# Loading the last block of w_out in a decode layer: four GpSimd transfers to ten of the DMA engines, in place of MLP rows and a side transfer

## The chip, the cores and the metric

The kernel runs on one core of one Trainium2 chip. The metric is the time of one execution on the device, in microseconds (us), as the median of several runs. Before the change it is 678.6 us, the median of three runs that lie between 678.34 and 678.68 us. A core has five instruction engines (TensorE or PE for matrix products, VectorE or DVE, ScalarE or ACT, GpSimd or POOL, SyncE or SP) and 16 DMA engines that carry all data between HBM and the on-chip memory SBUF.

## The reference, cut to what matters

One decode step: attention over a cached K and V, gated by a small MLP, both computed from the same normalised input.

```python
# B=8, D=512, Hq=32, Hkv=8, Sk=4096, Dh=128, Fh=896, one new position
xn = _layernorm(x, axis=-1)
s = _A_ref(xn, k_cache, v_cache, wq, wo)     # softmax(q k^T / sqrt(Dh)) v, then @ wo
z = gelu(xn @ w_in)                          # 512 -> 2*896
z1, z2 = z[..., :Fh], layernorm(z[..., Fh:])
g = silu((z1 * (w_sp * z2 + b_sp)) @ w_out)  # 896 -> 512
return x + s * g
```

All data are float32. The two caches hold 2 x 8 x 8 x 4096 x 128 numbers, 268 MB of the 291 MB that one execution reads.

## The kernel before, in words

**Buffers.** Three slots of 128 partitions x 16384 numbers, `slot_A`, `slot_B` and `slot_C` (8 MB each), take everything that is large. First `slot_B` takes wq, `slot_C` the MLP's weights and `slot_A` half of the first head's K. Then the eight heads follow (L645): for each, K in two halves into A and B, V in two halves into C and B. At the end wo goes into A in seven pieces, each smaller than the last or as large (`WO_PIECES`).

**Queues.** SP issues nearly all transfers, in program order: wq (L365), the side transfer (L371), then K, V and wo. An issue waits on SP until TensorE has freed the slot; the transfers themselves queue behind each other, so that there is as a rule a second one waiting when the first ends. ACT issues the input x in two parts (L362) and the MLP's weights (L368). GpSimd issues none. The hardware cuts a transfer over 128 partitions into rows, one for each partition, eight rows for each of the 16 DMA engines.

**The MLP's weights.** `w_in` (512 x 1792) and `w_out` (896 x 512) lie on the host as one array of 128 rows, `w_mlp`. `w_out` consists of `NB` = 7 blocks of 128 rows, each 512 columns; `LAST` is block 6. `w_mlp` holds w_in, the blocks 0 to 5, and of block 6 the first 256 columns: 10496 numbers in a row. The other 256 columns of block 6 come apart, as `w_ext`: 8 groups (`XG`) of 4 rows (`XR`), 32 rows of 1024 numbers (4 KB), which land on partitions 0 to 31 of `slot_C` behind the MLP's rows. So block 6's right half lies there in four chunks (`XC`) of 32 rows of w_out each.

**What uses them.** `mlp()` multiplies by w_in (L469), does gelu, norm and gate on VectorE, transposes the result u (L502) and multiplies by w_out (L514). For the right half of block 6, u's last columns are transposed once more in four chunks of 32 (L509), copied by VectorE (L510), and multiplied by the four chunks (L518). With the last of these products the MLP's use of `slot_C` ends: SP then issues the first V half into it (L596). VectorE copies y out of PSUM (L520).

**GpSimd** does little: a few constants at the start, a power for the first norm (L422) and one for the MLP's norm (L496), and for each head a copy of q (L543). Its program begins with one control instruction (`ISA`, in the table of its order below), before and after the change.

**Order.** Nothing is scheduled by a planner: each engine's instructions stand in the order in which the code issues them; a recorder (`Recorder`, `plan`) adds the waits on semaphores. A transfer with a key, such as `slots["C"]`'s, is waited for by TensorE at its first use; one without a key, such as the side transfer, has a semaphore of its own.

Of the kernel before, what the change touches and what calls it, by code (L numbers as in the profile page):

```python
# [15 lines left out]
P = 128  # L16
B, D = 8, 512
HKV, REP, S, DH = 8, 4, 4096, 128
NK = D // P
G = 4  # L20
J = S // (G * P)
R = 32
FH = 896
FQ = 256
NB = FH // P
# [11 lines left out]
E = 2  # L37
W = P // E
BANK = 512
XG, XR, XN = 8, 4, 256  # L40
XK = XG * XR
XC = P // XK
LAST = NB - 1


class Region:
# [297 lines left out]
        return self.rec.add(self.eng, "tensor_tensor", (out, a, b), {"op": ALU.subtract})  # L344


def gqa_gmlp_decode(real, x, kT, v, wq, wo, w_mlp, w_ext, out):
    nc = Recorder(real)

    def sb(name, shape, **kw):  # L350
        return real.alloc_sbuf_tensor(name, shape, F32, **kw).ap()

    def psum(name, shape):
        return real.alloc_psum_tensor(name, shape, F32).ap()

    slots = {n: sb(f"slot_{n}", [P, SLOT], align_bytes=ALIGN) for n in "ABC"}
    pbuf = sb("pbuf", [P, J * P])
    tbuf = sb("tbuf", [P, B * J * G * REP])
# [5 lines left out]

    nc.sync.dma_start(slots["B"], wq, key="B")  # L365
    wq_sb = slots["B"].rearrange("p (k n) -> p k n", k=NK)
    n_in, n_mlp = NK * 2 * FH, NK * 2 * FH + NB * D - XN
    nc.scalar.dma_start(slots["C"][:, :n_mlp], w_mlp, key="C")  # L368
    w_in_sb = slots["C"][:, :n_in].rearrange("p (k n) -> p k n", k=NK)
    ext = slots["C"][:XK, n_mlp:n_mlp + XC * XN]  # L370
    nc.sync.dma_start(ext, w_ext[:, :XR])  # L371
    w_ext_sb = ext.rearrange("p (c d) -> p c d", d=XN)

    def w_out_sb(j):
        return slots["C"][:, n_in + j * D:min(n_in + (j + 1) * D, n_mlp)]

    ident = sb("ident", [P, P])
    make_identity(nc, ident)
# [27 lines left out]
    def shift(t, i):  # L406
        lo = (E - 1 - i) * B
        return t[:, lo:lo + R]

    sc = psum("sc", [P, 2, 512])  # L410
    o_ps = [psum(f"o_ps{i}", [P, G, DH]) for i in range(2)]
    po = psum("po", [P, 512])[:, :B * REP]
    scr = [psum(f"scr{i}", [P, 512]) for i in range(3)]
# [6 lines left out]
    nc.vector.bn_aggr(mv, st)  # L420
    nc.vector.tensor_scalar(rstd[:, 0:1], mv[:, 1:2], EPS, None, op0=ALU.add)
    nc.gpsimd.tensor_tensor(rstd[:, 1:2], rstd[:, 0:1], neg_half[:B, 0:1], op=ALU.pow)  # L422
    nc.vector.tensor_scalar(xn, x_sb, mv[:, 0:1], rstd[:, 1:2], op0=ALU.subtract, op1=ALU.mult)
    pt = scr[0][:, :NK * B]
    for k in range(NK):
# [5 lines left out]
    for i in range(E):  # L431
        for g in range(G):
            lo = g * P + i * W
            nc.tensor.matmul(px[R * g:R * (g + 1), :W], shift(same8, i)[:B], x_sb[:, lo:lo + W],
                             start=(i == 0), stop=(i == E - 1))
# [21 lines left out]
    def mlp():  # L457
        zu = pbuf.rearrange("p (a f) -> p a f", f=FQ)
        z, u = zu[:, :2], zu[:, 2:]
        hT = tbuf[:, :2 * P].rearrange("p (a s) -> p a s", a=2)  # L460
        y_sb, e = tbuf[:, 2 * P:2 * P + D], zu[:, 2, :W]
        pz = scr[1]
        nc.vector.memset(pz, 0.0)
        for part in range(2):
            for k in range(NK):
                for g in range(G):
                    lo = g * FQ
                    n = min(FQ, FH - lo)
                    nc.tensor.matmul(pz[R * g:R * (g + 1), part * FQ:part * FQ + n], xnT[:, k, :],  # L469
                                     w_in_sb[:, k, part * FH + lo:part * FH + lo + n],  # L470
                                     start=(k == 0), stop=(k == NK - 1))
        zf, uf = z.rearrange("p a f -> p (a f)"), u.rearrange("p a f -> p (a f)")
        nc.vector.tensor_copy(zf, pz)
        nc.vector.tensor_mul(uf, zf, zf)
        nc.vector.tensor_scalar(uf, uf, 0.044715, 1.0, op0=ALU.mult, op1=ALU.add)
        nc.vector.tensor_mul(uf, uf, zf)
        nc.scalar.activation(uf, uf, AF.Tanh, scale=GELU_C)
        nc.vector.tensor_scalar(uf, uf, 1.0, 0.5, op0=ALU.add, op1=ALU.mult)
        nc.vector.tensor_mul(zf, uf, zf)

        def mean(src, pm, name):
            part_sum, t = sb(f"{name}_sum", [P, 1]), sb(name, [P, 1])
            nc.vector.tensor_reduce(part_sum, src, op=ALU.add, axis=AX.X)
            nc.tensor.matmul(pm, same_all, part_sum, start=True, stop=True)
            nc.vector.tensor_scalar(t, pm, 1.0 / FH, None, op0=ALU.mult)
            return t

        z1, z2 = z[:, 0, :], z[:, 1, :]
        mu = mean(z2, scr[0][:, :1], "mu")
        nc.vector.tensor_scalar(z2, z2, mu, None, op0=ALU.subtract)  # L490
        nc.vector.tensor_mul(u[:, 0, :], z2, z2)
        nc.vector.memset(u[(G - 1) * R:, 0, FH - (G - 1) * FQ:], 0.0)
        var = mean(u[:, 0, :], scr[2][:, :1], "var")
        nc.vector.tensor_scalar(var, var, EPS, None, op0=ALU.add)
        rs = sb("rs", [P, 1])
        nc.gpsimd.tensor_tensor(rs, var, neg_half, op=ALU.pow)  # L496
        nc.vector.tensor_scalar(z2, z2, rs, None, op0=ALU.mult)
        nc.vector.tensor_scalar(z2, z2, wb[:, 0:1], wb[:, 1:2], op0=ALU.mult, op1=ALU.add)
        nc.vector.tensor_mul(u[:, 1, :], z2, z1)
        th = scr[0][:, :2 * P]  # L500
        for a in range(2):
            nc.tensor.transpose(th[:, a * P:(a + 1) * P], u[:, 1, a * P:(a + 1) * P], ident)  # L502
        nc.vector.tensor_copy(hT.rearrange("p a s -> p (a s)"), th)
        low = R * (LAST // 2)
        hX = tbuf[:XK, 2 * P + D:2 * P + D + XC * R].rearrange("p (c r) -> p c r", r=R)
        tx = scr[2][:XK, :XC * R].rearrange("p (c r) -> p c r", r=R)
        for c in range(XC):
            lo = (LAST % 2) * P + c * XK
            nc.tensor.transpose(tx[:, c, :], u[low:low + R, 1, lo:lo + XK], ident[low:low + R, low:low + R])  # L509
        nc.vector.tensor_copy(hX, tx)  # L510
        for j in range(NB):
            g = j % G
            w_j = w_out_sb(j)
            nc.tensor.matmul(sc[R * g:R * (g + 1), 0, :w_j.shape[1]], hT[:, j % 2, R * (j // 2):R * (j // 2 + 1)],  # L514
                             w_j, start=(j < G), stop=(j + G >= NB and j < LAST))
        g = LAST % G
        for c in range(XC):
            nc.tensor.matmul(sc[R * g:R * (g + 1), 0, D - XN:], hX[:, c, :], w_ext_sb[:, c, :],  # L518
                             start=False, stop=(c == XC - 1))
        nc.vector.tensor_copy(y_sb, sc[:, 0, :])  # L520
        py = scr[2][:, :W]
        for i in range(E):
            for g in range(G):
                lo = g * P + i * W
                nc.tensor.matmul(py[R * g:R * (g + 1), :], shift(same8, i), y_sb[:, lo:lo + W],
                                 start=(i == 0), stop=(i == E - 1))
        nc.vector.tensor_scalar(e, py, -1.0, 87.0, op0=ALU.mult, op1=ALU.min)
        nc.scalar.activation(e, e, AF.Exp)
        nc.vector.tensor_scalar(e, e, 1.0, None, op0=ALU.add)
        nc.vector.reciprocal(e, e)  # L530
        nc.vector.tensor_mul(gate, py, e)
# [7 lines left out]
    p = pbuf.rearrange("p (j s) -> p j s", j=J)  # L539
# [101 lines left out]
    project_q(0)  # L641
    project_q(1)
    mlp()
    nc.meet("tensor")
    for h in range(HKV):  # L645
# [9 lines left out]
    for i in range(E):  # L655
        for g in range(G):
            lo = g * P + i * W
            nc.tensor.matmul(acc[R * g:R * (g + 1), :], shift(same8, i), part_sb[:, lo:lo + W],
                             start=False, stop=False)
# [43 lines left out]
```

## Time and profile before

The times of one execution, as the profiler took it:

| | |
|---|---|
| time of the profiled execution | 678.58 us (median of the three timed runs 678.6) |
| its span, first to last instruction | 677.3 us |
| bytes read from HBM | 290.74 MB, 429 GB/s over the span |
| TensorE (PE) busy | 374.1 us (55%) |
| VectorE (DVE) busy | 165.1 us (24%) |
| ScalarE (ACT), GpSimd (POOL) busy | 15.0 us, 4.4 us |
| mean granted TensorE clock | 0.773 |

How to read it: the span is the time between the first and the last instruction, and 1.3 us more lie around it. "DMA share" in the rows further down is the busy time of the transfers that began in a stretch, divided by the stretch and by 16, so 1.00 is all 16 engines at work; in a stretch shorter than a transfer it can be far above 1. From a stretch in which just one row of a transfer began, the row's time is therefore share x 16 x the stretch's length. Queue q1 in the page's list of queues is SP's, q10 is ACT's, q8 and q14 carry instructions and tables, not data.

### The profile page before, as it was taken

What the parts mean: (1) busy time and instruction counts of PE and PEld (TensorE: products, weight loads), DVE (VectorE), ACT (ScalarE), POOL (GpSimd) and SP (SyncE); (2) the same over time, 40 slices, a digit from 0 to 9 for tenths busy, and PEclk for the clock granted to TensorE, in tenths of its full rate; (3) what the DMA queues carried; (4) which work ended last, traced back from release to release, by engine and by line L of the source; (5) the groups of instructions that cost most, each with busy time, mean ns of one, the idle gap of its engine ahead of it and who ended that gap; (6) DMA issues with size and microseconds to landing.
All of it is one profiled execution on the core that took longest, in us unless ns stands there. A gap on an engine that the chain in (4) does not pass through costs nothing. (4 is left out here: it accounts for less than half of the span.)

```text
span 677.3 us, 6190 instructions
## 1 busy us (share of the span) xinstructions
PE 374.1 (55%) x2670; PEld 120.4 (18%) x2670; DVE 165.1 (24%) x262; ACT 15.0 (2%) x35; POOL 4.4 (1%) x22
## 2 busy tenths in 40 slices
PE   0084865446665454555754464655745356655576
PEld 0031221112211121111211121111211021111222
DVE  2014133301430033401431024401422024400451
ACT  0000000000000000000000000000000000000000
POOL 1000000000000000000000000000000000000000
PEclk9996767787876667887676778877667788876688
DMA  9999999999999999999999999999999999999997
GB/s 383 435 438 434 434 434 431 434 434 437 434 434 434 434 434 434 434 434 434 434 434 434 434 434 434 434 437 434 437 441 434 434 437 434 434 437 434 427 419 310
DMA packets 6270, 290.86 MB, mean 429 GB/s; under 512 B 840, under 2 KB 856, under 8 KB 1528
## 3 DMA queue, kind: packets, MB, share of 16 engines
q1 hardware_dynamic: 6088, 285.38, 97.4%
q10 hardware_dynamic: 176, 5.39, 1.8%
q8 instruction: 5, 0.08, 0.0%
q14 instruction: 1, 0.01, 0.0%
HBM read 290.74 MB, written 0.03 MB: 429 GB/s over the span
## 5 line engine op out<-in xcount | busy, mean ns | idle before, releaser
L550 PE MATMUL sc<-slot_B,qz 128*32 128x512 f32 x512 | 72.0, 725 | 70.9 <-PEq L550 70.9
L582 PE MATMUL o_ps<-slot_B,tbuf 128*16 128x512 f32 x512 | 75.3, 715 | 62.7 <-PEq L582 62.7
L550 PE MATMUL sc<-slot_A,qz 128*32 128x512 f32 x512 | 73.8, 741 | 45.6 <-PEq L550 45.6
L582 PE MATMUL o_ps<-slot_C,tbuf 128*16 128x512 f32 x512 | 75.7, 732 | 12.6 <-PEq L582 12.6
L584 DVE TENSOR_TENSOR o_all<-o_ps,diag 128x512 f32<-128x512 f32 x64 | 44.2, 691 | 133.2 <-DVEq L584 133.2
L554 DVE TENSOR_REDUCE nm<-sc 128x1 f32<-128x1024 f32 x8 | 9.8, 1225 | 266.2 <-DVEq L554 266.2
L585 DVE TENSOR_REDUCE o_sb<-o_all 128x128 f32<-128x512 f32 x64 | 67.7, 1058 | 9.3
L550 PEld LDWEIGHTS sc<-slot_B,qz 128*32 128x32 f32 x512 | 19.9, 130 | 122.8 <-issue 122.8
L550 PEld LDWEIGHTS sc<-slot_A,qz 128*32 128x32 f32 x512 | 20.2, 133 | 92.7 <-issue 92.7
L588 PE MATMUL po<-fold,o_sb 128*128 128x4 f32 x128 | 24.2, 259 | 18.8 <-PEq L588 17.4
L588 PEld LDWEIGHTS po<-fold,o_sb 128*128 128x128 f32 x128 | 19.9, 195 | 74.3 <-issue 74.3
L582 PEld LDWEIGHTS o_ps<-slot_B,tbuf 128*16 128x16 f32 x512 | 13.4, 105 | 90.5 <-issue 90.1
L582 PEld LDWEIGHTS o_ps<-slot_C,tbuf 128*16 128x16 f32 x512 | 15.5, 112 | 53.8 <-issue 53.5
L572 PE MATMUL scr<-ident,pbuf 128*128 128x128 f32 x64 | 15.5, 424 | 13.4 <-PEq L572 13.4
L447 PE MATMUL scr<-slot_B,xnT 128*32 128x512 f32 x64 | 9.7, 761 | 19.1 <-PEq L447 19.1
L572 PEld LDWEIGHTS scr<-ident,pbuf 128*128 128x128 f32 x64 | 12.6, 224 | 13.8 <-issue 13.8
L555 ACT ACTIVATE pbuf<-sc,nm 128x1024 f32<-128x1024 f32 x8 | 8.9, 1113 | 273.5 <-DVEq L554 273.5
L573 DVE COPY tbuf<-scr 128x512 f32<-128x512 f32 x16 | 11.1, 691 | 12.4 <-DVEq L573 12.4
L558 PE MATMUL scr<-ident,nm 128*1 128x128 f32 x8 | 2.2, 269 | 13.7 <-PEq L558 13.7
L449 DVE TENSOR_SCALAR pbuf<-scr 128x512 f32<-128x512 f32 x2 | 1.4, 691 | 28.0 <-PE scr L447 28.0
L609 PE MATMUL sc<-slot_A,oT 128*8 128x512 f32 x48 | 7.8, 729 | 0.8 <-DMA slot_A<-in_wo 0.8
L565 PE MATMUL scr<-wl,same 128*128 128x1 f32 x16 | 3.6, 297 | 8.0 <-PEq L565 8.0
(105 smaller groups left out, 83.4 us busy)
## 6 DMA issues: line engine op xcount, KB each, us to landing
slot_B<-in_v SPq DMA_DIRECT2D x1, 6144.0 KB, 25.4
slot_C<-in_w_mlp ACTq DMA_DIRECT2D x1, 5248.0 KB, 35.8
slot_A<-in_wo SPq DMA_DIRECT2D x1, 3584.0 KB, 36.4
slot_B<-in_v SPq DMA_DIRECT2D x1, 2048.0 KB, 28.3
slot_A<-in_wo SPq DMA_DIRECT2D x1, 2048.0 KB, 40.8
slot_A<-in_wo SPq DMA_DIRECT2D x2, 768.0 KB, 42.9
slot_A<-in_wo SPq DMA_DIRECT2D x1, 512.0 KB, 44.3
slot_A<-in_wo SPq DMA_DIRECT2D x2, 256.0 KB, 44.6
```

Of the source, the lines that this page charges most:

```text
L447: nc.tensor.matmul(pq[R * g:R * (g + 1), :], xnT[:, k, :], wq_sb[:, k, lo:lo + REP * DH], start=(k == 0), stop=(k == NK - 1))
L550: nc.tensor.matmul(sc[R * g:R * (g + 1), c, :], qz[:, b * R:(b + 1) * R], k_sb[:, i, c, g, :], start=(b == 0), stop=(b == B - 1))
L554: nc.vector.tensor_reduce(nm, sc, op=ALU.max, axis=AX.XY, negate=True)
L555: nc.scalar.activation(p.rearrange("p j s -> p (j s)"), sc.rearrange("p c s -> p (c s)"), AF.Exp, bias=nm, accum_out=l)
L565: nc.tensor.matmul(tot, same_all, wl, start=True, stop=True)
L572: nc.tensor.transpose(t[:, j * P:(j + 1) * P], p[:, 4 * c + j, :], ident)
L573: nc.vector.tensor_copy(pT[:, :, 4 * c:4 * c + 4].rearrange("p b j (g r) -> p (j g) b r", g=G), t.rearrange("p (m b r) -> p m b r", b=B, r ...
L582: nc.tensor.matmul(of[R * c:R * c + G * REP, :], pT[:, b, j, :], v_unit[:, j], start=(j < G), stop=(j >= J - G))
L584: nc.vector.tensor_mul(o_all[b % 2], o, diag[:, :, None].to_broadcast([P, G, DH]), after=after)
L585: nc.vector.tensor_reduce(o_sb[b % 2], o_all[b % 2].rearrange("p g d -> p d g"), op=ALU.add, axis=AX.X)
L588: nc.tensor.matmul(po[:, b * REP:(b + 1) * REP], o_sb[b % 2], fold, start=True, stop=True)
L609: nc.tensor.matmul(part[R * r:R * r + B, :], oT[:, h, r, :], wo_sb[:, m, :], start=(m < REP), stop=(m >= FOLDED - REP))
```

## The change

The side transfer `w_ext` goes, and with it the extra transposes, the copy and the products in four chunks. `w_mlp` now holds w_in and the blocks 0 to 5 only, 10240 numbers in a row. Block 6 comes whole (128 rows of 512 numbers, 2 KB each), by four transfers that GpSimd issues behind its first power, with three tiny transfers between them that move 8 or 12 numbers into unused columns:

```diff
+SPRAY = [(2, 13), (2, 2, 2), (2, 12), (1, 2, 3), (3, 13), (1, 2, 3), (3, 13)]
+SG = sum(t[0] for t in SPRAY if len(t) == 2)
+SR = 14
...
-    n_in, n_mlp = NK * 2 * FH, NK * 2 * FH + NB * D - XN
+    n_in, n_mlp = NK * 2 * FH, NK * 2 * FH + LAST * D
...
-    ext = slots["C"][:XK, n_mlp:n_mlp + XC * XN]
-    nc.sync.dma_start(ext, w_ext[:, :XR])
+    def load_last():
+        row, group, spare = 0, 0, n_mlp + D
+        for k, n, *dummy in SPRAY:
+            if not dummy:
+                nc.gpsimd.dma_start(slots["C"][row:row + k * n, n_mlp:n_mlp + D], w_last[group:group + k, :n])
+                row, group = row + k * n, group + k
+            else:
+                m = dummy[0]
+                to = slots["C"][:n, spare:spare + 3 * m].rearrange("p (a c) -> p a c", c=3)
+                src = w_last[:m, SR - 1, :3 * n].rearrange("p (a c) -> p a c", c=3)
+                nc.gpsimd.dma_start(to[:, :, :2], src[:, :, :2])
+                spare += 3 * m
...
     nc.gpsimd.tensor_tensor(rstd[:, 1:2], rstd[:, 0:1], neg_half[:B, 0:1], op=ALU.pow)
+    load_last()
...
         for j in range(NB):
             g = j % G
...
-        g = LAST % G
-        for c in range(XC):
-            nc.tensor.matmul(sc[R * g:R * (g + 1), 0, D - XN:], hX[:, c, :], w_ext_sb[:, c, :],
-                             start=False, stop=(c == XC - 1))
+            nc.tensor.matmul(sc[R * g:R * (g + 1), 0, :], hT[:, j % 2, R * (j // 2):R * (j // 2 + 1)],
+                             w_out_sb(j), start=(j < G), stop=(j + G >= NB))
```

An entry (k, n) of `SPRAY` is a transfer of k groups of n rows; the source is laid out on the host as groups of 14 rows (`SR`), so that its slowest dimension has k entries. The first thus moves 2 groups of 13 rows, the second 2 of 12, the third and fourth 3 of 13 each: ten groups and 128 rows in all. An entry (k, n, m) is a tiny transfer.

On GpSimd, from the power of the first norm to the first copy of q. Before (`rs`, `var`, `rstd`, `neg_half` are small operands of the norms, `qz` and `qT` hold q):

```order
L422 TENSOR_TENSOR rstd<-rstd,neg_half 8x1
L496 TENSOR_TENSOR rs<-var,neg_half 128x1
L543 COPY qz<-qT 128x8x4 x8
```

After, the same place:

```order
L432 TENSOR_TENSOR rstd<-rstd,neg_half 8x1
L375 DMA slot_C<-in_w_last 26x1x512
L381 DMA slot_C<-in_w_last 2x2x2
L375 DMA slot_C<-in_w_last 24x1x512
L381 DMA slot_C<-in_w_last 2x3x2
L375 DMA slot_C<-in_w_last 39x1x512
L381 DMA slot_C<-in_w_last 2x3x2
L375 DMA slot_C<-in_w_last 39x1x512
L507 TENSOR_TENSOR rs<-var,neg_half 128x1
L542 COPY qz<-qT 128x8x4 x8
```

The seven transfers stand between the two powers; none of them waits for anything.

On TensorE, the end of the MLP, from the transposes of u to the products that sum y (`scr`, `sc` are PSUM banks, `tbuf` holds the transposed u). Before:

```order
L502 MATMUL scr0<-ident,pbuf 128x128 x2
L509 MATMUL scr2<-ident,pbuf 32x32 x4
L514 MATMUL sc<-slot_C,tbuf 32x512 x6
L514 MATMUL sc<-slot_C,tbuf 32x256
L518 MATMUL sc<-slot_C,tbuf 32x256 x4
L525 MATMUL scr2<-tbuf,same8 32x64 x8
```

After:

```order
L513 MATMUL scr0<-ident,pbuf 128x128 x2
L517 MATMUL sc<-slot_C,tbuf 32x512 x7
L524 MATMUL scr2<-tbuf,same8 32x64 x8
```

Nine instructions (L509, the half-width product, L518) have become one full-width product. Its data now come from GpSimd's transfers, and it waits for all four of them.

On SP, the first transfers of the program, before and after:

```order
L365 DMA slot_B<-in_wq 128x16384
L371 DMA slot_C<-in_w_ext 32x1x1024
L591 DMA slot_A<-in_kT 128x16384
L591 DMA slot_B<-in_kT 128x16384
L596 DMA slot_C<-in_v 128x16384
```

```order
L365 DMA slot_B<-in_wq 128x16384
L590 DMA slot_A<-in_kT 128x16384
L590 DMA slot_B<-in_kT 128x16384
L595 DMA slot_C<-in_v 128x16384
```

The side transfer is gone from SP's queue, and the first V load into `slot_C` (L595) now also waits for the three tiny transfers.

More of the change, by code (lines that the diff above doesn't have):

```diff
@@ L39 @@
 BANK = 512
-XG, XR, XN = 8, 4, 256
-XK = XG * XR
-XC = P // XK
 LAST = NB - 1
+SPRAY = [(2, 13), (2, 2, 2), (2, 12), (1, 2, 3), (3, 13), (1, 2, 3), (3, 13)]
+SG = sum(t[0] for t in SPRAY if len(t) == 2)
+SR = 14
 class Region:
@@ L344, in tensor_sub, with gqa_gmlp_decode @@
         return self.rec.add(self.eng, "tensor_tensor", (out, a, b), {"op": ALU.subtract})
-def gqa_gmlp_decode(real, x, kT, v, wq, wo, w_mlp, w_ext, out):
+def gqa_gmlp_decode(real, x, kT, v, wq, wo, w_mlp, w_last, out):
     nc = Recorder(real)
@@ L366, in gqa_gmlp_decode @@
     wq_sb = slots["B"].rearrange("p (k n) -> p k n", k=NK)
-    n_in, n_mlp = NK * 2 * FH, NK * 2 * FH + NB * D - XN
+    n_in, n_mlp = NK * 2 * FH, NK * 2 * FH + LAST * D
     nc.scalar.dma_start(slots["C"][:, :n_mlp], w_mlp, key="C")
     w_in_sb = slots["C"][:, :n_in].rearrange("p (k n) -> p k n", k=NK)
-    ext = slots["C"][:XK, n_mlp:n_mlp + XC * XN]
-    nc.sync.dma_start(ext, w_ext[:, :XR])
-    w_ext_sb = ext.rearrange("p (c d) -> p c d", d=XN)
+    def load_last():
[10 more added lines that the diff above has]
+                spare += 3 * m
     def w_out_sb(j):
-        return slots["C"][:, n_in + j * D:min(n_in + (j + 1) * D, n_mlp)]
+        return slots["C"][:, n_in + j * D:n_in + (j + 1) * D]
     ident = sb("ident", [P, P])
@@ L503, in mlp @@
         nc.vector.tensor_copy(hT.rearrange("p a s -> p (a s)"), th)
-        low = R * (LAST // 2)
-        hX = tbuf[:XK, 2 * P + D:2 * P + D + XC * R].rearrange("p (c r) -> p c r", r=R)
-        tx = scr[2][:XK, :XC * R].rearrange("p (c r) -> p c r", r=R)
-        for c in range(XC):
-            lo = (LAST % 2) * P + c * XK
-            nc.tensor.transpose(tx[:, c, :], u[low:low + R, 1, lo:lo + XK], ident[low:low + R, low:low + R])
-        nc.vector.tensor_copy(hX, tx)
         for j in range(NB):
             g = j % G
-            w_j = w_out_sb(j)
-            nc.tensor.matmul(sc[R * g:R * (g + 1), 0, :w_j.shape[1]], hT[:, j % 2, R * (j // 2):R * (j // 2 + 1)],
-                             w_j, start=(j < G), stop=(j + G >= NB and j < LAST))
-        g = LAST % G
-        for c in range(XC):
-            nc.tensor.matmul(sc[R * g:R * (g + 1), 0, D - XN:], hX[:, c, :], w_ext_sb[:, c, :],
-                             start=False, stop=(c == XC - 1))
+            nc.tensor.matmul(sc[R * g:R * (g + 1), 0, :], hT[:, j % 2, R * (j // 2):R * (j // 2 + 1)],
+                             w_out_sb(j), start=(j < G), stop=(j + G >= NB))
         nc.vector.tensor_copy(y_sb, sc[:, 0, :])
@@ L683 @@
         c(w_out.transpose(1, 0, 2)).reshape(P, NB * D)], axis=1)
-    w_ext = w_out[LAST, :, D - XN:].reshape(XC, XG, XR, XN).transpose(1, 2, 0, 3).reshape(XG, XR, XC * XN)
-    w_ext = np.concatenate([w_ext, np.zeros((XG, 1, XC * XN), np.float32)], axis=1)
+    w_last = np.zeros((SG, SR, D), np.float32)
+    row, group = 0, 0
+    for m, n, *dummy in SPRAY:
+        if not dummy:
+            w_last[group:group + m, :n] = w_out[LAST, row:row + m * n].reshape(m, n, D)
+            row, group = row + m * n, group + m
     arrays = {
@@ L691 @@
         "wo": c(c(A_wo).reshape(HKV * REP, P, D).transpose(1, 0, 2)).reshape(P, SLOT),
-        "w_mlp": c(w_mlp[:, :NK * 2 * FH + NB * D - XN]),
-        "w_ext": w_ext,
+        "w_mlp": c(w_mlp[:, :NK * 2 * FH + LAST * D]),
+        "w_last": w_last,
     }
```

## The prediction

> **What bounds the kernel now.** I read the page's head first, its row of the DMA share and its list of queues (packets, MB, share of the 16 engines).
>
> ```profile
> span 677.3 us, 6190 instructions
> ...
> DMA  9999999999999999999999999999999999999997
> ...
> q1 hardware_dynamic: 6088, 285.38, 97.4%
> q10 hardware_dynamic: 176, 5.39, 1.8%
> q8 instruction: 5, 0.08, 0.0%
> q14 instruction: 1, 0.01, 0.0%
> ```
>
> The DMA engines are busy in every slice but the last; no other engine is above 55%. The kernel takes as long as its transfers. Next the chain that ended last, in order of time (start, length, what):
>
> ```profile
> 629.99 44.67 DMA slot_A<-in_wo
> 674.66 0.04 issue
> 674.70 0.47 PE sc L617 x16
> ```
>
> The last piece of wo lands at 674.66; what follows, TensorE's last products first, is short and fixed. But 16 engines bring that piece, and it counts as landed when the last of them is done. So the third view is of the end, cut finely (stretch, its length, busy times of five engines, clock, DMA share, GB/s):
>
> ```profile
> 672.10:672.40 0.30, 0.24 (x16) 0.25 (x20) 0.00 (x1) 0.00 (x0) 0.00 (x0) 1.00 0.97 382
> 672.40:672.65 0.25, 0.25 (x35) 0.25 (x28) 0.00 (x0) 0.00 (x0) 0.00 (x0) 1.00 0.68 262
> 672.65:672.90 0.25, 0.25 (x32) 0.25 (x24) 0.00 (x0) 0.00 (x0) 0.00 (x0) 1.00 0.57 221
> 672.90:673.40 0.50, 0.36 (x28) 0.19 (x16) 0.00 (x0) 0.00 (x0) 0.00 (x0) 1.00 0.35 135
> 673.50:673.60 0.10, 0.09 (x6) 0.10 (x10) 0.00 (x0) 0.00 (x0) 0.00 (x0) 1.00 0.37 143
> 673.60:673.80 0.20, 0.20 (x21) 0.20 (x24) 0.00 (x0) 0.00 (x0) 0.00 (x0) 1.00 0.27 102
> 673.80:674.00 0.20, 0.20 (x27) 0.20 (x15) 0.00 (x0) 0.00 (x0) 0.00 (x0) 1.00 0.19 72
> 674.00:674.20 0.20, 0.20 (x21) 0.14 (x13) 0.00 (x0) 0.00 (x0) 0.00 (x0) 1.00 0.08 31
> 674.20:674.30 0.10, 0.10 (x16) 0.10 (x10) 0.00 (x0) 0.00 (x0) 0.00 (x0) 1.00 0.05 20
> 674.30:674.40 0.10, 0.10 (x15) 0.03 (x4) 0.00 (x0) 0.00 (x0) 0.00 (x0) 1.00 0.01 0
> ```
>
> 382 GB/s from 16 engines is about 24 from one, so GB/s over 24 to 25 counts the engines still at work: all until 672.4, some 9 to 10 until 672.9, then 5 to 6, 4, 3, 1, 1 and none. Eleven engines have nothing left after 673.1; five go on, and stop at about 673.6, 673.75, 673.95, 674.1 and 674.3. Counted back from the last, the five end at -0.7, -0.55, -0.35, -0.2 and 0, the eleven between -2.0 and -1.2. The kernel ends with the slowest engine, so **what counts is which engine has how much to move**. Perfect balance would end near the mean of these, -1.2 (eleven at -1.6, five at -0.36), and that is the most that any shift of load can give.
>
> Why are five late? Rows around the fetches on q8 and q14, each stretch so short that one row began in it (time = share x 16 x length); the last two are from the list of queues in 102.68 to 102.70 and in 673.42 to 673.43:
>
> ```profile
> 95.52:95.53 0.01, 0.01 (x2) 0.01 (x2) 0.00 (x0) 0.00 (x0) 0.00 (x0) 0.50 1.93 819
> 95.70:95.71 0.01, 0.01 (x2) 0.01 (x1) 0.01 (x1) 0.00 (x0) 0.00 (x0) 0.50 15.11 6554
> 95.82:95.83 0.01, 0.01 (x2) 0.01 (x1) 0.01 (x1) 0.00 (x0) 0.00 (x0) 0.50 18.44 6554
> 103.55:103.56 0.01, 0.01 (x4) 0.00 (x0) 0.01 (x1) 0.00 (x0) 0.00 (x0) 1.00 18.55 6554
> ...
> q8 instruction: 1, 0.02, 274.7%
> ...
> q8 instruction: 1, 0.02, 677.5%
> ```
>
> A usual 64-KB row takes 15.11 x 0.16 = 2.42 us. A fetch on q8 takes 2.747 x 0.32 = 0.88 us, and the row behind it 18.55 x 0.16 = 2.97, so 0.55 more: 1.43 us on one engine. The fetch on q14 takes 0.31 and costs the next row 0.53: 0.84. Of the five on q8 one begins only at 673.42. Four and one before the end, five late engines: I take each for one.
>
> **The change part by part.** Sizes of rows: a row of w_mlp, two rows of w_ext together, and a completion (4 bytes):
>
> ```profile
> 7.30:7.31 0.01, 0.00 (x0) 0.00 (x0) 0.00 (x0) 0.00 (x0) 0.00 (x0) 1.00 9.70 4198
> 34.59:34.60 0.01, 0.01 (x8) 0.01 (x4) 0.00 (x0) 0.00 (x0) 0.00 (x0) 1.00 1.99 819
> 208.45:208.46 0.01, 0.00 (x0) 0.00 (x0) 0.00 (x0) 0.00 (x0) 0.00 (x0) 0.50 0.06 0
> ```
>
> That is 1.55 us for 42.0 KB, 0.16 us for 4 KB and 9 ns. A 2-KB row is read at the end, 0.27 x 3.2 us / 10 rows = 0.086; I take 84 ns.
>
> - Removed everywhere: 1 KB from each of eight rows of w_mlp, 8 x 1.55 x 1/41 = 0.30 us for each engine.
> - Removed with w_ext: 32 rows in 8 groups of 4. I take one group for one engine, so on eight engines 4 x 0.16 = 0.64 us. The spread of the eleven (-2.0 to -1.2) fits: six without, five with. Eight engines thus lose 0.94, eight lose 0.30.
> - Added: a group of 13 rows on each of ten engines, 13 x 0.084 = 1.09 us (two have 12). Seven completions, 0.06 us; the tiny rows I put with them.
>
> By these prices the last two, -0.2 and 0, had w_ext and a q8 fetch (-1.6 to -1.2, plus 1.43). The other three are two without w_ext (-2.0 to -1.7, plus 1.43: -0.6 to -0.3) and one with it and the small fetch (plus 0.84). So of the late ones three had w_ext, two had not. **If the six engines that get no group include those five**, the ends become: late with w_ext 0 - 0.94 = -0.94; late without -0.35 - 0.30 = -0.65; loaded, without w_ext before, -1.7 - 0.30 + 1.09 = -0.91; loaded, with it, -1.2 - 0.94 + 1.09 = -1.05. The last is at -0.65, with 0.06 for completions **-0.6 us**. Whether they are the six no row shows. Between the groups the tiny transfers leave out two, one, one, and behind the last two: third, fourth, seventh, eleventh, fifteenth and sixteenth, counted from the first. If the count starts where w_ext's eight start, three lie among these eight and three outside, which agrees with three and two. The bounds, if not: a late engine with w_ext that gets a group ends at 0 + 0.15, one without at -0.35 + 0.79 = +0.44.
>
> The Trainium skill, "DMA: Bandwidth & Descriptors", section "Why a DMA increments its semaphore by 16 and not by 1", says that the number of engines is the largest up to 16 that divides the slowest dimension of both sides, the lowest-numbered ones for transfers from SP, consecutive ones from a moving cursor for GpSimd's. By it w_ext took eight and the four transfers 2, 2, 3 and 3, and the sum stays; no run here shows the cursor.
>
> On the instruction side I cost nothing. TensorE loses its share of 1.91 us of L518 and frees `slot_C` earlier:
>
> ```profile
> 65.25 0.95 PE L514 MATMUL sc<-slot_C,tbuf 128*32 128x512 f32 x2
> ...
> 66.13 1.91 PE L518 MATMUL sc<-slot_C,tbuf 32*32 32x256 f32 x8
> 68.07 0.33 SPq L596 DMA_DIRECT2D slot_C<-in_v  x1
> ...
> L591 SPq DMA_DIRECT2D slot_B<-in_kT x1: 328/328/328, 44.9 to 44.9; - x1
> ...
> DMA to landing us min/median/max: 30.3/30.3/30.3
> ```
>
> SP issues the next load at 68.07, while the load before it, of 44.9, keeps engines busy until 75.2. The cover is 7 us less the start of a transfer, so neither 2 us earlier nor some later moves the end. GpSimd issues behind its power, at 12.33, and its next instruction is wanted at 59.56:
>
> ```profile
> 11.79 0.54 POOL L422 TENSOR_TENSOR rstd<-rstd,neg_half 8x1 f32<-8x1 f32 x1 [9.35 <-DVE rstd L421]
> ...
> 59.56 0.57 POOL L496 TENSOR_TENSOR rs<-var,neg_half 128x1 f32<-128x1 f32 x1 [47.23 <-DVE var L494]
> ...
> 1.19 0.82 SPq L371 DMA_DIRECT2D slot_C<-in_w_ext  x1
> ```
>
> What an issue costs GpSimd is not shown; SP's take 0.33 to 0.82 us, so seven take 2.3 to 5.7 and end by 18.1; even 6 us each would be hidden.
>
> **The rivals.** *No shift to speak of* (the late engines get groups, or GpSimd spreads the rows evenly: 8 rows on each engine, 0.67 us, so 0 - 0.27 or -0.35 + 0.37): +0.44 at most, 678.5 to 679.0. For it: nothing shows the cursor. Against: three and two.
>
> *Slower: bubbles.* Each fetch on q8 or q14 cost the 64-KB row behind it 0.53 to 0.55 us beyond its own time. If a transfer on GpSimd's new queue does the same wherever it arrives, and all seven arrive on all 16 engines, that is 7 x 0.53 = 3.7 us, less 0.6: 681.7. It makes the kernel slower by 0.2% (1.36 us) from four arrivals on the slowest engine. Against: the small rows of q10 and the completions among q1's leave the rows about them at 2.42. The same section of the Trainium skill says that for GpSimd's transfers all 16 engines post a completion, whatever the shape; by it all seven arrive everywhere. No trace here shows that queue.
>
> *Late rows.* If an engine takes one row of each queue in turn, GpSimd's 13 rows and up to seven completions wait behind 64-KB rows: 3.97 us a turn while w_mlp lasts (to about 37), 2.5 after it. From 18.1 on that is 37 + 15.2 x 2.5 = 75 us. The last product (0.95), the issue (0.33) and 1 us of start put the next rows at 77.3, 2.1 after 75.2: 680.1. With 14 turns the rows are in by 60 and cost nothing. It hurts from rows later than 72.9. For it: two rows of x, issued at 0.73, were there only at 10.64:
>
> ```profile
> 10.64 0.68 DVE L419 BATCH_NORM_STATS2 st<-pbuf 8x6 f32<-8x512 f32 x1 [6.98 <-DMA pbuf<-in_x]
> ```
>
> The Trainium skill, same page, section "Queues, rings and completion order", says that an engine takes a whole packet, about 9 to 17 descriptors, before it turns to the next queue. By that a group comes in a turn or two and nothing is late; x's rows, on a queue of another kind, speak against it.
>
> **How the numbers follow.** The sum is against the profiled execution's own 678.58 us (span 677.3 and 1.3 around it), which is the median of the runs shown, 678.6: 678.58 - 0.6 = **678.0**. Chances: forecast 0.58; no shift 0.22; bubbles 0.10; late rows 0.07; 0.03 for a gain beyond balance, for which I see no mechanism. 0.2% is about what a measurement of this kernel can tell from no change, and neither the forecast nor the first rival reaches it: within 0.2% has 0.80, slower 0.17, faster 0.03. The range reaches from 677.3 (the whole -1.2) to 680.2 (no shift, late rows, up to four bubbles); outside lie the larger part of the bubbles and the gain.
>
> **What would show it.** Right: at the end the engines stop closer together, within 0.8 us (-1.45 to -0.65) instead of 2.0, but for a sixth one that gets no group and has no fetch, and wo lands near 674.0; a new queue has 128 rows of 2 KB before 35 us; the rows behind them take 2.42. Wrong: rows of 2.9 us behind the new queue's (bubbles); the last product of w_out after 66 us with SP's next issue behind it (late rows); five engines still late at the end (no shift). A fetch that comes to another engine in the changed program would break the forecast too.

## The result, and the profile after

The changed kernel takes **686.97 us** (median of five runs, 686.62 to 689.25) against 678.6 before. The ratio is 1.0132, with a 95% interval of 1.012 to 1.0143: 8.4 us slower. The forecast was 678.0, the range 677.3 to 680.2, and slower had a chance of 0.17. So the sign and the size were both wrong. One execution of e7_sp below, its profiled one, took 702.38 us in a slower state that no other run here shows; it is left out of that run's time, and its trace is read for counts only.

The page of the profiled execution after (its time is 688.03 us, the span and 1.3 around it, so 9.45 more than the 678.58 of the one before):

```profile
span 686.7 us, 6174 instructions
...
DMA  9999699999999999999999999999999999999997
...
DMA packets 6822, 290.87 MB, mean 424 GB/s; under 512 B 1356, under 2 KB 1372, under 8 KB 2080
## 3 DMA queue, kind: packets, MB, share of 16 engines
q1 hardware_dynamic: 6048, 285.25, 96.5%
q10 hardware_dynamic: 176, 5.26, 1.8%
q0 software_dynamic: 592, 0.27, 0.1%
```

Two things are new. The row of the DMA share has a 6 where it had only nines: in the fifth slice (69 to 86 us) the engines that bound the kernel were not all at work. And there is a queue q0, GpSimd's, with 592 packets for 0.27 MB. The change wanted 128 rows there.

What happened ahead of that slice shows in the timeline (start, length, engine, line, what; in brackets the idle time before and who ended it):

```profile
12.27 0.78 POOL L375 DMA_DIRECT2D slot_C<-in_w_last  x1
...
15.46 0.63 POOL L381 DMA_DIRECT2D slot_C<-in_w_last  x1
43.54 0.65 POOL L375 DMA_DIRECT2D slot_C<-in_w_last  x1 [27.45 <-issue]
43.82 0.33 SPq L590 DMA_DIRECT2D slot_B<-in_kT  x1
...
63.34 3.63 PE L517 MATMUL sc<-slot_C,tbuf 128*32 128x512 f32 x12 [0.52 <-DVE tbuf L514]
...
77.27 1.89 PE L517 MATMUL sc<-slot_C,tbuf 128*32 128x512 f32 x2 [10.30 <-DMA slot_C<-in_w_last]
...
79.24 0.33 SPq L595 DMA_DIRECT2D slot_C<-in_v  x1
```

TensorE does the first twelve products of w_out at 63.34, within a microsecond of before, and then stands for 10.30 us, because GpSimd's rows of the last block are not there. They were issued from 12.27 on and landed near 77. The last two products end at 79.16, and only then can SP issue the next load into `slot_C`: at 79.24, where before it was 68.07. The load ahead of it (K's second half into B, 43.82) was done at 76.6. What the engines did meanwhile (stretch, length, busy times of five engines, clock, DMA share, GB/s):

```profile
70.00:75.00 5.00, 0.00 (x0) 0.00 (x0) 0.00 (x0) 0.00 (x0) 0.00 (x0) 0.58 0.64 250
75.00:80.00 5.00, 1.95 (x6) 0.24 (x10) 0.69 (x1) 0.00 (x0) 0.00 (x0) 0.50 0.01 2
80.00:85.00 5.00, 2.95 (x28) 1.03 (x32) 1.20 (x4) 0.26 (x1) 0.00 (x0) 0.50 1.12 419
```

In the second row next to nothing begins. What the wait cost is best read in a longer stretch, by GB/s, since that counts both idle engines and slower rows. First before, then after:

```profile
70.00:105.00 35.00, 27.21 (x196) 9.29 (x200) 8.93 (x18) 1.41 (x3) 0.00 (x0) 0.77 1.01 436
```

```profile
70.00:105.00 35.00, 20.12 (x150) 6.12 (x150) 4.63 (x13) 1.66 (x4) 0.00 (x0) 0.71 0.82 336
```

Of 35 us the engines lost 35 x (1 - 336/436) = **8.0 us** here. That is most of the 9.45 us that this execution lost; the grain of this reading is about half a microsecond, since e5_plain below, as fast as the kernel before, has 443 GB/s in the same stretch. The chain at the end is as it was, only later: wo lands at 684.12 instead of 674.66.

```profile
638.87 45.25 DMA slot_A<-in_wo
684.12 0.04 issue
684.16 0.47 PE sc L616 x16
```

**Why the rows came late.** Count the packets. The page's 592 are 16 engines x 37, and 37 can be accounted for. If an engine takes two 2-KB rows as one packet of 4 KB, a group of 13 rows is seven packets, a group of 12 six, and every transfer has one packet more at its end: 8 + 7 + 8 + 8, and 2 for each of the three tiny ones, is 37. But there are only ten groups for 16 engines. So on every engine outside a transfer's groups there must be as many packets, without data worth the name. Their sizes say the same. The kernel with no transfer on GpSimd (e5_plain, below) has this row on its page:

```profile
DMA packets 6230, 290.86 MB, mean 430 GB/s; under 512 B 832, under 2 KB 848, under 8 KB 1488
```

That is 592 fewer packets, and 524 fewer of under 512 B. The other 68 are eight groups of 13 rows with seven each, and two of 12 with six: 8 x 7 + 2 x 6 = 68. The 524 are fillers, completions (the small packet at a transfer's end) and the tiny transfers' data. The trace's records give 490 of them 4 or 8 bytes, the other 34 at most 48; the 68 are 60 packets of 4,096 bytes and 8 of 2,048.

And an engine takes one packet of q0 for each 64-KB row. In the list of queues between 40 and 70 us (packets, MB, share):

```profile
q1 hardware_dynamic: 209, 12.65, 99.6%
q0 software_dynamic: 208, 0.07, 1.0%
```

208 packets of q0 beside 209 of q1 (193 rows of 64 KB by the MB, 16 completions): turn by turn. So each of the 37 packets waits for a row of about 2.4 us, and for about 4 us while w_mlp's queue is at work as well. That they wait for turns, and not for GpSimd or for their own transfer, shows when the 64-KB rows run out, between 73.7 and 76.1 us. In 73.7 to 76.3 the list of queues has

```profile
q0 software_dynamic: 247, 0.13, 19.7%
```

That is 247 packets in 2.6 us, after 208 in the 30 us shown above.

The Trainium skill, "DMA: Bandwidth & Descriptors", section "SWDGE vs HWDGE vs iDMA", says of a packet that it is at most 4096 bytes preferably, and that it is the unit at whose end an engine turns to another queue; the two rows to a packet and the turns here agree with it. The section of the Trainium skill that the prediction named, on queues and rings, has about 9 to 17 descriptors in a packet; here a packet of data held one or two rows, so that figure does not fit this queue.

### The profile page after: what moved, and what is told of

Read it like the earlier page. It is cut to its first block, busy times and chain, and to the rows that moved or that the text cites. A ratio compares the mean times of both kernels' runs of the same rounds, so it can differ in the third digit from the quotient of the medians.

```text
span 686.7 us, 6174 instructions
## 1 busy us (share of the span) xinstructions
PE 373.9 (54%) x2658; PEld 120.2 (18%) x2658; DVE 164.9 (24%) x261; ACT 15.0 (2%) x35; POOL 8.8 (1%) x29
## 5 line engine op out<-in xcount | busy, mean ns | idle before, releaser
L549 PE MATMUL sc<-slot_A,qz 128*32 128x512 f32 x512 | 73.7, 740 | 46.5 <-PEq L549 46.5
L517 PE MATMUL sc<-slot_C,tbuf 128*32 128x512 f32 x14 | 5.5, 1060 | 10.8 <-DMA slot_C<-in_w_last 10.3
L542 POOL COPY qz<-qT 128x32 f32<-128x32 f32 x8 | 1.7, 208 | 539.3 <-ACT oT L638 461.6
```

Of the source, the lines that this page charges most:

```text
L517: nc.tensor.matmul(sc[R * g:R * (g + 1), 0, :], hT[:, j % 2, R * (j // 2):R * (j // 2 + 1)], w_out_sb(j), start=(j < G), stop=(j + G >= NB))
L549: nc.tensor.matmul(sc[R * g:R * (g + 1), c, :], qz[:, b * R:(b + 1) * R], k_sb[:, i, c, g, :], start=(b == 0), stop=(b == B - 1))
```

## The experiments

Each is one edit of the kernel before or of the changed one, timed beside the kernel before on the same chip (678.47 to 678.55 us there). None leaves out a part of the computation; some add transfers or reductions of which nothing uses the result.

**e1_ring.** GpSimd held its fourth large transfer for 27.45 us in the changed kernel. Was that what made it late? The memory for its descriptors is made four times as large:

```diff
-dynamic_dma_scratch_size=1024
+dynamic_dma_scratch_size=4096
```

> The changed kernel with four times the room for GpSimd's descriptors (4096 instead of 1024 bytes a partition), nothing else. Late rows (each GpSimd transfer puts small rows on all 16 engines, an engine takes one packet of them behind each 64-KB row, 37 turns in all): the fourth large transfer is issued at about 16 us instead of 43.5, but the last product of w_out still starts at 75 to 78 us, and the time stays at 686 to 688 us. Ring too small (the fourth transfer was held back until 43.5 and that alone made its rows late): rows in before 66 us, no wait, 678 to 679 us.

Measured: 686.97 us (686.41 to 688.74), ratio 1.0132 (1.0113 to 1.0151). Its timeline:

```profile
15.91 0.66 POOL L375 DMA_DIRECT2D slot_C<-in_w_last  x1
...
77.75 1.89 PE L517 MATMUL sc<-slot_C,tbuf 128*32 128x512 f32 x2 [10.93 <-DMA slot_C<-in_w_last]
...
79.73 0.33 SPq L595 DMA_DIRECT2D slot_C<-in_v  x1
```

That transfer is issued 27.6 us earlier and is there no sooner. The hold was real and free: the packets wait on the engines' side, not for GpSimd. The expectation of late rows holds, that of a ring too small does not.

**e2_one.** The same block by one transfer, 16 groups of 8 rows, and no tiny ones: 8 rows are four packets, and one at the end, 5 turns.

```diff
-SPRAY = [(2, 13), (2, 2, 2), (2, 12), (1, 2, 3), (3, 13), (1, 2, 3), (3, 13)]
+SPRAY = [(16, 8)]
```

> The changed kernel with one GpSimd transfer of all 128 rows (16 groups of 8) in place of the seven. Late rows: five turns on each engine, rows in by 36 to 40 us, the last product does not wait, SP issues the next load into slot_C at 66 to 68 us; 678.3 to 679.0 us. Traffic (the rows of GpSimd's queue slow the 64-KB rows beside them): about a seventh of the changed kernel's surplus stays, 679 to 680. Ring too small: as late rows.

Measured: 679.39 us (679.14 to 679.98), ratio 1.0015 (1.0005 to 1.0024).

```profile
q0 software_dynamic: 80, 0.26, 0.1%
```

```profile
65.04 3.64 PE L517 MATMUL sc<-slot_C,tbuf 128*32 128x512 f32 x14 [0.52 <-DVE tbuf L514]
...
68.72 0.33 SPq L595 DMA_DIRECT2D slot_C<-in_v  x1
```

80 is 16 x 5. All fourteen products run in one piece, SP's issue comes within 0.7 us of before (68.07), and most of the loss is gone. Some 0.9 us are left, which late rows alone (678.3 to 679.0) did not expect and traffic (679 to 680) did.

**e3_traffic.** The kernel before, with the change's seven GpSimd transfers into a tile of their own, which nothing waits for (`load_last` is the change's, with `spare_sb` in place of slot C; a memset of the tile on VectorE near the end is off the chain that ends last):

```diff
+    spare_sb = sb("spare_sb", [P, D + 24])
...
     nc.gpsimd.tensor_tensor(rstd[:, 1:2], rstd[:, 0:1], neg_half[:B, 0:1], op=ALU.pow)
+    load_last()
```

> The kernel before, with its side transfer, and beside it the change's seven GpSimd transfers into a buffer that nothing reads until the end. Late rows: nobody waits for them, so the time is that of before plus 256 KB (0.6 us) and the slower 64-KB rows until 75 us (about 0.9): 679 to 680.5 us. Traffic: the 3 us by which the changed kernel's 64-KB rows were slower in all come here too: 681.5 to 683 us.

Measured: 681.75 us (681.14 to 681.94), ratio 1.0047 (1.003 to 1.0064). SP's issue into slot C comes at 69.68. The long stretch:

```profile
70.00:105.00 35.00, 26.15 (x194) 9.06 (x198) 8.47 (x18) 1.66 (x4) 0.00 (x0) 0.76 1.01 424
```

No engine idles, yet 3.3 us are lost. The bytes, which here come on top, are 8 rows an engine on average, 0.67 us by the prediction's price; 2.6 us remain. Most of them sit in the 64-KB rows that take turns with q0's packets. In the list of queues between 40 and 70 us, q1 has, first in the kernel before, then here, then in e8_k4spare further down:

```profile
q1 hardware_dynamic: 209, 12.65, 97.4%
```

```profile
q1 hardware_dynamic: 206, 12.45, 98.0%
```

```profile
q1 hardware_dynamic: 207, 12.52, 100.5%
```

By the MB these are 193, 190 and 191 rows of 64 KB. Share x 16 x 30 us, divided by the rows, is 2.42 us a row before, 2.48 here and 2.53 in e8_k4spare. Summed over the whole trace and divided by 16, the 64-KB rows take 1.6 us more than before, and the small packets' own time is 0.3; where the other 0.7 us are is not shown. A single pair in the changed kernel (each stretch with just one packet in it; time = share x 16 x length):

```profile
53.13:53.14 0.01, 0.00 (x0) 0.00 (x0) 0.01 (x1) 0.00 (x0) 0.00 (x0) 1.00 0.06 1
53.14:53.15 0.01, 0.00 (x0) 0.00 (x0) 0.01 (x1) 0.00 (x0) 0.00 (x0) 1.00 16.24 6554
```

The first is a filler of 9 ns, the second a 64-KB row that begins behind it: 16.24 x 0.16 = 2.60 us instead of 2.42. Not every row beside a filler is that slow. Spread over 37 packets, the 2.6 us lost are 0.07 each.

**e4_k4.** The changed kernel with four transfers of 4 groups of 8 rows and no tiny ones: 4 x 5 = 20 turns, the number that the prediction's rival of late rows had counted.

```diff
-SPRAY = [(2, 13), (2, 2, 2), (2, 12), (1, 2, 3), (3, 13), (1, 2, 3), (3, 13)]
+SPRAY = [(4, 8), (4, 8), (4, 8), (4, 8)]
```

> The changed kernel with four GpSimd transfers of 4 groups of 8 rows and no tiny ones: five turns each, 20 in all, all issued by 16 us and within the room for descriptors. Late rows: rows in at 70 to 74 us, the last product starts then, SP's next load is issued at 72 to 76 us, 678.5 to 681 us, and one turn takes about 2.45 us once w_mlp is in. Ring too small: nothing is held back, so no wait, 678 to 679 us.

Measured: 681.92 us (680.02 to 682.95), ratio 1.0046 (1.0031 to 1.0062); 320 packets, 16 x 20. Their sizes in the trace are 64 of 4,096 bytes, 192 of 8 and 64 of 4: for each transfer 16 of data, four fillers on each of the 12 engines outside its groups, and 16 completions.

```profile
71.29 1.89 PE L517 MATMUL sc<-slot_C,tbuf 128*32 128x512 f32 x2 [5.41 <-DMA slot_C<-in_w_last]
...
73.21 0.33 SPq L595 DMA_DIRECT2D slot_C<-in_v  x1
```

The number of turns sets when the rows are there: 71 instead of 77, as expected; the time is above the 681 that was expected at most. SP's issue still comes ahead of the end of the load before, and by the trace's packets the engines stand still for only 0.1 us at this place and 0.3 at the next slot. So the larger part of the 3.4 us left is not idle time.

**e5_plain.** The changed kernel without any transfer on GpSimd: block 6 whole in w_mlp's rows, w_ext gone.

```diff
-    n_in, n_mlp = NK * 2 * FH, NK * 2 * FH + LAST * D
+    n_in, n_mlp = NK * 2 * FH, NK * 2 * FH + NB * D
...
-    load_last()
```

> The changed kernel without any transfer on GpSimd: all of block 6 comes in the rows of w_mlp, w_ext is gone too. My theory (the slots wait for late rows, and traffic on GpSimd's queue slows the 64-KB rows beside it): both are gone, so the loss is gone; by the prediction's own prices each engine gets 0.30 us more of w_mlp and eight lose 0.64 of w_ext, so the last end moves by about -0.05 us: 678.4, between 678.1 and 678.8, and no engine idle between 70 and 80 us. Rival (some of the loss comes from the rest of the edit: one longer w_mlp row, products of w_out in one pass without the two transposes): above 679.8.

Measured: 678.47 us (678.28 to 679.01), ratio 1.0001 (0.9992 to 1.001). The rest of the edit costs nothing that can be measured; all of the loss comes with GpSimd's transfers.

**e6_twice.** As e3_traffic, with the seven transfers twice and the larger memory for descriptors of e1_ring:

```diff
-    load_last()
+    load_last(0)
+    load_last(D + 24)
```

> The kernel before with GpSimd's seven transfers twice into a tile of their own that nothing waits for (ring of descriptors four times as long). Each engine gets 74 turns instead of 37, and 0.67 us more of bytes. Theory (each packet of GpSimd's queue costs the 64-KB row beside it about 0.07 us): 678.5 + 2 x 0.67 + 74 x 0.07 = 685.0, between 684 and 686. Rival (the cost comes once, from the queue's being in use at all): 678.5 + 2.6 + 1.3 = 682.4. Rival (only bytes count and the 3.3 us of the single set came from elsewhere): 681.8 + 0.7 = 682.5 as well, but then without 64-KB rows above 2.42 us behind the point where the first set ends.

Measured: 685.23 us (684.79 to 685.47), ratio 1.01 (1.0084 to 1.0115); 1184 packets of q0, 16 x 74. 685.0 was expected of a price for each packet, 682.4 of a price paid once. 6.7 us less 1.34 for bytes are 5.3 us over 74 turns, 0.07 each, as in e3: the same mix of packets twice costs twice as much.

**e7_sp.** The change's four large transfers issued by SP, without the tiny ones:

```diff
-                nc.gpsimd.dma_start(slots["C"][row:row + k * n, n_mlp:n_mlp + D], w_last[group:group + k, :n])
+        nc.sync.dma_start(slots["C"][row:row + k * n, n_mlp:n_mlp + D], w_last[group:group + k, :n])
```

> The change's four large transfers issued by SP, on the queue of all other loads, with no tiny ones. No rows wait behind 64-KB rows of another queue, so no slot is freed late (last product near 66 us, next issue of SP by 69), and no engine idles. But all four start at the same engine: two engines get 51 rows of 2 KB, 51 x 0.084 = 4.3 us, less the 0.3 to 0.9 that they lose. Theory of the prediction that the kernel ends with the slowest engine (ends of -2.0 to 0 before): +1.4 to +4.0, 680 to 682.5. Rival (16 engines share a load so that 4 us on two of them are made up elsewhere): 678.1 to 678.8.

Measured: 681.96 us (681.87 to 682.93), ratio 1.0056 (1.0041 to 1.0072). The loss of 3.4 us lies inside the range that the slowest engine's share gives, and far from "made up elsewhere". It agrees with the view that the slowest engine sets the end. The page has 6186 packets on q1, 138 more than in e5_plain: the 128 rows and ten small ones, 2 + 2 + 3 + 3. So SP's transfers put nothing on the engines outside their groups. That the four all began on the same engine isn't shown by a row.

**e8_k4spare.** The four transfers of e4_k4 into the tile of e3_traffic (the diff is that of e3, with e4's `SPRAY`).

> The kernel before with GpSimd's four transfers of 4 groups of 8 rows (20 turns on each engine) into a tile of their own that nothing waits for. Theory (the same transfers into slot C gave 681.9 by slowing 64-KB rows, not by the wait): 681.4 to 682.4. Rival (a price of 0.07 us per turn as in the seven transfers: 678.5 + 0.67 + 20 x 0.07): 680.5, and the remaining 1.4 us of the kernel with slot C came from the late last product.

Measured: 681.2 us (680.58 to 681.67), ratio 1.0036 (1.0023 to 1.005). It falls between the two expectations, 681.4 to 682.4 and 680.5. Less 0.67 for bytes it is 2.0 us for 20 turns; by the interval 0.05 to 0.14 a turn. The rows of q1 shown with e3 agree: 2.53 us, a larger surcharge than there. So 0.07 is not the price of any packet, only of that mix. With slot C (e4) no bytes are added, and 3.4 us were lost, 1.4 more; but the intervals of the two overlap (0.9 to 2.7 and 2.1 to 4.2), so that something else was at work in e4 is not shown by the times.

**e9_late, e10_cover, e11_cover3.** No queue of GpSimd at all: e5_plain, with ten, five or three reductions on VectorE ahead of the copy that w_out's products wait for. They only make SP's issue late.

```diff
+        for _ in range(10):
+            nc.vector.tensor_reduce(spare_sb[:, 1024:], spare_sb[:, :1024], op=ALU.add, axis=AX.X)
         nc.vector.tensor_copy(hT.rearrange("p a s -> p (a s)"), th)
```

> The kernel without any GpSimd transfer, with ten VectorE reductions of a spare tile (about 1.2 us each, an estimate from the reductions of 128x1024 at L573) ahead of the copy that w_out's products wait for: SP's next load into slot C is issued about 12 us later, near 79, as in the changed kernel, but no queue of GpSimd is in use. Theory (the larger part of the loss, some 5 us, is the engines' idle time between the end of the load before, mean near 74.2, and that issue plus 1 us): engines idle from 74 to 80, and the time is 678.5 + (issue + 1.0 - 74.2) + up to 0.7 for the slower start of a load: 684 to 685.5. Rival (the idle stretch is made up later, and the change's loss is all traffic): 678.2 to 679.5.

> The same with five reductions: SP's issue comes about 6 us later than without them, near 73, still ahead of the end of the load before. Theory and the prediction's cover (an issue up to about 7 us later costs nothing): 678.2 to 679.0, no idle stretch. Rival (every microsecond by which a slot is freed later costs time): 680 to 684.

> The same with three reductions: SP's issue near 70.6. In the two runs before this one the first rows of the new load began 1.0 to 1.1 us after the issue, and the engines had run dry from 73.4 on; the issue near 73.1 cost 2.3 us, a stretch of idle time and a first row of 3.16 us instead of 2.42, once there and once more at the next load of a slot. Theory (the cover ends about 1 us before the first engine runs dry, so at an issue near 72.3): at 70.6 nothing is lost, 678.2 to 679.0. Rival (a slot freed later costs in proportion, 2.3 us for 6.2): 679.6 to 680.2.

| run | SP's issue into slot C | us (median, from, to) | ratio, 95% |
|---|---|---|---|
| e5_plain | 66.88 | 678.47 (678.28 to 679.01) | 1.0001 (0.9992 to 1.001) |
| e11_cover3 | 69.69 | 678.77 (678.33 to 679.15) | 1.0005 (0.9995 to 1.0014) |
| e10_cover | 73.09 | 680.75 (678.73 to 682.19) | 1.0033 (1.0023 to 1.0043) |
| e9_late | 78.44 | 686.99 (686.72 to 687.44) | 1.0129 (1.0112 to 1.0146) |

The issue times are those of the profiled executions. In e9_late the wait alone, without a packet of GpSimd's, costs as much as the whole change. Its issues and its long stretch:

```profile
78.44 0.33 SPq L582 DMA_DIRECT2D slot_C<-in_v  x1
...
98.90 0.33 SPq L582 DMA_DIRECT2D slot_B<-in_v  x1
```

```profile
70.00:105.00 35.00, 22.09 (x163) 6.62 (x164) 9.61 (x18) 1.67 (x4) 0.00 (x0) 0.70 0.81 330
```

35 x (1 - 330/436) = 8.5 us, all that the run lost, and 2.6 us more than the 684.4 that the expectation's formula gives for an issue at 78.44. Three things make up most of the difference. Summed over the trace's packets, the engines run dry at 73.4 on average, not at 74.2, and stand still for 6.1 us at this stop instead of the formula's 5.2. The second issue shows that the delay goes on to the next slot: in e5_plain that issue came at 86.04; here it comes at 98.90, while 8 MB that began near 79.4 are done by 99 at 430 GB/s, and the engines stand still for another 0.5 us. And the first row of each engine after a stop is slow, both times. In e10_cover 16 rows begin in one microsecond:

```profile
74.00:75.00 1.00, 0.50 (x16) 0.26 (x12) 0.23 (x1) 0.17 (x1) 0.00 (x0) 0.50 3.16 1049
```

1049 GB/s for 1 us are 16 rows of 64 KB, with a mean of 3.16 us instead of 2.42. The engines of this run had gone dry one after another between 73.1 and 74.9. So an issue at 73.09, ahead of all these ends, already costs 2.3 us in the median, though the ten runs spread over 3.5 us; the expected cover of about 7 us failed here.

## Why the prediction was wrong

- **The step that failed** is in the part on the instruction side: "The cover is 7 us less the start of a transfer, so neither 2 us earlier nor some later moves the end." The sum had GpSimd's rows arrive in time, and so no term for a wait of TensorE ("On the instruction side I cost nothing"). The rows came 10 us too late for it, SP's issue 11 us, and such a delay alone is enough for the loss (e9_late: 8.5 us with the wait and no traffic; the changed kernel: 8.4).
- **The cover itself** was overrated too. With an issue at 69.69 nothing that can be measured is lost, at 73.09 there are 2.3 us. The 75.2 was the last engine's end; in e10_cover the first ones run dry from 73.1, a load's first rows begin about 1 us behind its issue, and they are slower by 0.7. A second stop at the next slot follows.
- **The rival of late rows** had the mechanism, one packet of GpSimd's queue between two 64-KB rows, and the sign by which it could be told (last product after 66 us with SP's next issue behind it). It was mis-sized. It counted 13 rows and 7 completions, 20 turns. It is 37: two rows go into one turn, but the turns of all seven transfers, those of other engines' groups too, pass through every engine. At the 2.5 us that it gave a turn, 4.8 turns by 37 us and 32.2 behind it would end at 37 + 32.2 x 2.5 = 117.5 us; in e3_traffic, where the engines don't run dry, the last of the transfers lands near 106. In the changed kernel the rows came at 77 only because the 64-KB rows ran out between 73.7 and 76.1. That the rival's 75 us lies near 77 is luck. With 37 turns, and the 64-KB rows at an end at 75.2, the rival would have given an issue near 79 and, by the prediction's own prices, 80.2 - 75.2 = 5.0 more, 683.6; the second stop and slower rows are the larger part of the rest.
- **"Seven completions, 0.06 us; the tiny rows I put with them"** failed in the same way: they are 524 small packets, some 33 an engine. On their own (e3, e6) q0's packets cost 0.07 us each, 2.6 us for the seven transfers, most of it in slower 64-KB rows. So the rival of bubbles was right that arrivals cost rows beside them, with 37 arrivals at 0.07 instead of seven at 0.53. In the changed kernel this is not added to the wait (8.4 in all, not 8.5 + 2.6), since rows that are slowed ahead of 75 us use time in which the engines would have stood still. The traces bear this out: SP's issue comes 0.8 us later than in e9_late, yet the engines stand still for 5.5 us at the first stop instead of 6.1. For the changed kernel's profiled execution the sum over all packets, for the mean engine and against before, is 5.5 + 0.4 us at the two stops, 2.9 in slower 64-KB rows (2.0 in e9_late against e5_plain, without traffic) and 1.0 in q0's packets, less 0.5 for what SP and ACT no longer bring: 9.3 of the 9.45 us.
- **"What an issue costs GpSimd is not shown ... hidden"**: seven issues took 0.6 to 0.8 us each, and the hold of 27.45 us at the fourth large one was hidden as well (e1_ring).
- **The balance of the engines**, on which the forecast rested, did not get its trial. All engines stop and start again near 80 us, so what an engine carried before is forgotten. At the end the GB/s of the changed kernel still fall over some 2 us:

```profile
682.00:682.50 0.50, 0.50 (x46) 0.50 (x43) 0.00 (x0) 0.00 (x0) 0.00 (x0) 1.00 0.49 188
682.50:683.00 0.50, 0.48 (x37) 0.35 (x27) 0.00 (x0) 0.00 (x0) 0.00 (x0) 1.00 0.25 94
683.00:683.50 0.50, 0.50 (x32) 0.46 (x32) 0.00 (x0) 0.00 (x0) 0.00 (x0) 1.00 0.21 66
683.50:684.00 0.50, 0.45 (x26) 0.27 (x16) 0.00 (x0) 0.00 (x0) 0.00 (x0) 1.00 0.04 16
```

  That is some eight engines at work, then four, three and one, so the gathering of the ends within 0.8 us is not there. Whether the engines without a group are the late ones stays open. e7_sp fits the arithmetic, 51 rows on one engine for 3.4 us. That w_ext used eight engines is borne out: without it (e5_plain) q1 has 40 packets fewer, 32 rows and eight small ones. And e5_plain, where w_ext's eight engines are relieved and nothing is put in its place, is at 1.0001: by the prediction's prices -0.05 us, too small to be seen.
- **Still open**: the 0.9 us of e2_one are 0.18 for each of its five turns, more than the 0.07 of e3 and e6 (by the interval from 0.3 us, 0.07 a turn). Taken with the 0.10 of e8's twenty turns, the price of a packet falls as the fillers grow in number; e2, e8 and e3 each have about four packets of data an engine, and whether those cost more than fillers no run tests. Also open is what slows the rows of e4_k4 beyond those of e8_k4spare (2.57 against 2.53 us between 40 and 70 us).

No version here beats the kernel before; e5_plain equals it.

## What to carry to other kernels

Ask of a small transfer not how many bytes it moves but how many turns it takes behind large rows, and how late it may be: 256 KB cost 0.9 us as one transfer over all 16 engines, and 8.4 as seven over few. Where DMA bounds a kernel, the issue that refills a slot must come before the first engine runs dry by more than the start of a transfer, about 1 us here; an issue 3.4 us ahead (69.69, against 73.1) cost nothing that could be measured, one at that moment 2.3. And a late slot can make the next one late as well. A term that rests on "it arrives in time" needs its arrival worked out first, by the same means as the rivals.

## What was not expected of the hardware

- A GpSimd transfer over few engines puts as many packets on all the others: 592 = 16 x 37 and 320 = 16 x 20, 192 of the 320 being fillers of 8 bytes. SP's transfers of the same shape put none there (e7_sp).
- An engine takes one packet of that queue, two rows of 2 KB at most, for each row of 64 KB: 208 beside 209 in 30 us.
- Small packets of 9 ns cost far more than their own time: 2.6 us for 37 turns, 5.3 for 74, and rows of 64 KB beside them take 2.48 us on average instead of 2.42.
- An engine's first row after a stop takes 3.16 us instead of 2.42 (e10_cover).
- GpSimd's issue was held for 27.45 us with the smaller memory for descriptors, and not at all with four times as much.
